# Batch 0's second token pair by seven products, one sink product for two heads, and a new order: windowed attention with sinks before a squared-ReLU layer pair

## The chip, the cores and the metric

The kernel runs on one core of a Trainium2 chip. The time is the device time in microseconds (us) of one execution; medians of runs are compared. The engines are called PE (TensorE: products; PEld: its weight loads), DVE (VectorE), ACT (ScalarE), POOL (GpSimd) and SP (SyncE, which here issues transfers).

## The reference

```python
batch, n_heads, seq, head_dim = (4, 8, 768, 64)
n_sink, window = (4, 128)

scores = scale * q @ k.T                       # per batch and head, scale = 1/sqrt(64)
keep = (column < n_sink) | (0 <= row - column < window)
a = softmax(where(keep, scores, -1e9))
x = (a @ v)                                    # -> [batch * seq, heads * 64] = [3072, 512]
h = x @ w_in                                   # [3072, 2048]
out = (relu(h) ** 2) @ w_out                   # [3072, 512], float32
```

(The lines are shortened from the reference; q, k and v are float32 of [4, 8, 768, 64].)

Attention is banded: a row sees 128 columns behind it and the first four columns of its batch, the sinks. Then come two dense layers with a squared ReLU between them.

## The kernel before

**Tiling.** A batch has 768 tokens, that is 6 tiles of 128 (t = 0 to 5), taken as 3 pairs (s or u = 0 to 2). Heads are taken in 4 pairs (m = 0 to 3), two of them at a time. Products are in bf16, sums in fp32 in the PSUM banks.

**Attention** (`attention`, from line 562). Queries and keys are turned, for batches 0 and 1 on PE (L642), for 2 and 3 by transposing transfers on SP (L596). Scores are products with 64 rows of contraction (L749), keys by queries, two heads in the two halves of the PE array. ACT takes the exponent into `expm` (L769); DVE or POOL masks the band's triangles (L778, L781, L360). The sinks' scores for all heads are one small group of products (`pk`, L708), and their exponents lie in `es`: heads in groups of four rows, so that one 128-row operand holds all heads. `vs` holds, for each head, the sinks' values (and a one for the row sum) in that head's rows and zero elsewhere. In `values` (L797 to L819) each head and token tile gets up to three products into 65 columns of a bank: previous tile, own tile, and, for t >= 2, the sinks (L815). Column 65 is the softmax's sum; DVE divides (L833, L834) into `xn_sb`. PE or a transfer turns that into `xT`, the input of the dense layers (L866 and its copies, L848).

**First layer** (`layer1`, L884). 16 blocks of 128 of the 2048 inner columns; products at L895 into `pm`, ReLU into `r` on ACT (L906) or DVE (L908), square into `gT` on DVE (L917) or ACT (L915).

**Second layer.** It exists in two forms, each for a pair of token tiles (256 tokens by 512 output columns, contraction 2048):
- `layer2` (L921): plain, 2 tiles by 16 blocks = 32 products of 512 columns (L936), then two copies of 128x512 to `osb`.
- `layer2_fast` (L981): one step of Winograd's form of Strassen's scheme. The pair is a 2 by 2 block matrix (tile by inner half), w_out another (inner half by column half). Seven block products of 8 products of 256 columns each (L1047) take the place of eight. Four sums of the left operand are made on DVE (L1005: s1 to s4; s3 in place in `gT`), four of w_out once for the kernel (`weight_sums`, L964, L977), and the results are combined by additions on DVE (L1072, L1088, L1095) and copies on ACT or DVE.

In the kernel before, pairs 0 and 1 of batch 0 go by `layer2` (in four parts by inner columns, `by_part=True`, L1193) and the other ten pairs by `layer2_fast`.

**The order of the work.** Nothing is ordered by the text of the program. Each step (a group of products, a copy, a load) is an `op` of a `Plan` (L152), with the engines that it may take, its planned cost on each, what it comes after and which buffers it takes and frees. `Plan.run` (L183) is a list scheduler: again and again it picks, of the ops that are ready, the one with the smallest planned start plus its own `lag`, and then the smallest `key`, gives it to the engine where it ends first, and emits it. A producer on another engine counts as ready LATENCY after its planned end (L222). `place` (L170) then moves the ops of a group, such as ('l2', b, u), by PLACES (shift of the key, scale of the key, lag), and single ops by NUDGES, which names them by their number in the list of ops (shift of the key, lag). So a changed number anywhere can change the order in all five queues. Loads keep their order within a queue (`follow`). Op 25 is the load of the third quarter of w_in, 24 and 26 those of the second and the fourth.

**Buffers.** The PSUM has two pools of two buffers each, `att` and `den` (L289); `sg` has four buffers for the sums of the fast form.

Of the kernel before, what the change touches and what calls it, by code (L numbers as in the profile page):

```python
# [16 lines left out]
LATENCY = 0.135  # L17
# [5 lines left out]
    ('att', 0, 0): (3.3, 1.08, 0.18), ('att', 0, 1): (3.285, 0.47, 0.38), ('att', 0, 2): (-0.2, 1.41, -0.24),  # L23
    ('att', 1, 0): (-1.415, 2.2, -0.42), ('att', 1, 1): (-0.385, 1.02, -0.22), ('att', 1, 2): (6.08, 1.06, 0.36),
    ('att', 2, 0): (-0.225, 0.25, -0.64), ('att', 2, 1): (-1.615, 1.17, -0.58), ('att', 2, 2): (0, 1.02, -0.06),
    ('att', 3, 0): (-0.075, 1.08, 0.1), ('att', 3, 1): (-0.04, 1.04, 0.04), ('att', 3, 2): (1.235, 0.72, 0.98),
    ('ev', 0, 2): (-0.16, 1.15, 0.78), ('ev', 1, 0): (0.585, 0.56, -0.48), ('ev', 1, 1): (0.47, 1.11, 0.24),
    ('ev', 1, 2): (-0.095, 1.18, 0.08), ('ev', 2, 0): (-0.22, 0.93, 0.28), ('ev', 2, 1): (0.015, 1.02, -0.46),
    ('ev', 2, 2): (1.345, 0.4, 1.32), ('ev', 3, 1): (-0.155, 1, 0.08), ('ev', 3, 2): (-0.055, 1.28, -0.44),
    ('l1', 0, 0): (-0.035, 1.27, 0), ('l1', 0, 1): (0.18, 0.85, 0.08), ('l1', 0, 2): (-0.6, 1.31, -0.4),  # L30
    ('l1', 1, 0): (4.96, 0.3, 0.74), ('l1', 1, 2): (0.265, 1.41, -0.28), ('l1', 2, 0): (-0, 0.59, 0.5),
    ('l1', 2, 2): (0.1, 1.22, -0.12), ('l1', 3, 0): (0.075, 0.91, 0.48), ('l2', 0, 0): (0.055, 0.81, 0.38),
    ('l2', 0, 1): (0.435, 1.16, 0), ('l2', 0, 2): (0.16, 1.12, -0.1), ('l2', 1, 0): (1.05, 0.56, -0.96),
    ('l2', 1, 1): (-0.425, 1.06, -0.1), ('l2', 1, 2): (-0.18, 1.03, 0.2), ('l2', 2, 0): (-0.115, 0.96, 0.58),
    ('l2', 2, 1): (2.185, 1.21, 1.32), ('l2', 2, 2): (2.75, 1, 0.74), ('l2', 3, 0): (-0.765, 0.25, 2.4),
    ('l2', 3, 1): (0.08, 0.81, 0.18), ('l2', 3, 2): (0.23, 1.94, 2.82), ('prep', 0, 0): (2.165, 1.2, -0.5),
    ('prep', 0, 1): (0.115, 1.01, -0.24), ('prep', 1, 0): (0.05, 0.87, 0.08), ('prep', 1, 1): (0.84, 1.23, 0.54),
    ('prep', 2, 0): (-0.005, 0.96, 0.24), ('prep', 3, 0): (-0.045, 1.08, 1.16),
    ('sink', 0, 0): (0.015, 1.11, -0.04), ('sink', 0, 1): (0, 1.12, -0.06), ('sink', 1, 0): (-0.225, 1.01, -0.06),
    ('sink', 3, 0): (-0.565, 0.62, 0.5), ('sum', 0, 2): (-0.14, 0.68, -0.34), ('sum', 1, 0): (-1.615, 0.44, -1.74),  # L40
    ('sum', 1, 1): (0.645, 0.91, -1.4), ('sum', 1, 2): (0.34, 1.45, 0.14), ('sum', 2, 0): (-0.655, 1.85, 0.06),
    ('sum', 2, 1): (-0.24, 1, 0.18), ('sum', 2, 2): (0.405, 1.27, 0.3), ('sum', 3, 0): (0.25, 2.36, 0.94),
    ('sum', 3, 2): (0.185, 1.17, 1.74), ('turn', 0, 0): (-0.56, 2.1, -0.62), ('turn', 0, 1): (0.11, 0.94, -0.14),
    ('turn', 0, 2): (-0.205, 1.01, 0.02), ('turn', 1, 0): (-0.2, 0.94, -0.02),
    ('turn', 1, 1): (-0.345, 1.33, -0.42), ('turn', 1, 2): (1.765, 2.5, -2.14), ('turn', 2, 0): (0, 1.05, 0),
    ('turn', 2, 1): (-0.26, 1.09, -0.3), ('turn', 3, 0): (-0.06, 1.05, -0.44), ('turn', 3, 1): (0.075, 0.56, 0.64),
    ('turn', 3, 2): (0, 1, 0.14), ('val', 0, 0): (0.345, 0.45, -0.28), ('val', 0, 1): (0.69, 0.58, -0.46),
    ('val', 0, 2): (-0.09, 0.78, -0.08), ('val', 1, 0): (-2.595, 0.7, 0.22), ('val', 1, 1): (0.035, 1.14, 0.06),
    ('val', 1, 2): (-0.65, 0.98, 0.64), ('val', 2, 0): (-1.11, 0.59, -1.94), ('val', 2, 1): (0.755, 0.42, -0.3),
    ('val', 2, 2): (-0.425, 1.6, -0.06), ('val', 3, 0): (0.1, 1.17, 0.6), ('val', 3, 1): (0.805, 0.25, 0.74),  # L50
    ('val', 3, 2): (0.105, 0.92, 2.28), ('wt', 0): (-0.205, 0.82, -0.32),
}
NUDGES = {
    4: (-0.022, 0.56), 16: (0, 0.14), 17: (-0.211, -0.38), 18: (0.48, -1.62), 19: (0, 0.4), 20: (0.364, -0.58),
    21: (0.004, 0.16), 22: (0.02, 0), 23: (0.016, 0.18), 24: (-0.06, -0.78), 25: (0.35, 1.84), 26: (-0.106, 0.66),
    27: (0.014, -0.64), 29: (-0.004, 0.86), 30: (0, 0.42), 31: (0.013, 0), 33: (-0.009, 0), 34: (-0.094, 0.5),
    36: (-0.027, 0.16), 37: (0.188, 0.08), 38: (-0.052, 0), 39: (-0.269, -0.82), 40: (-0.004, 0),
    41: (-0.419, 0.34), 42: (0.398, -2.86), 43: (0.134, -0.1), 44: (0.027, 0.14), 45: (0.009, 0), 46: (0.123, 0.66),
    47: (0.073, 0.9), 49: (0, 0.1), 51: (-0.102, -0), 52: (-0.278, -0.06), 53: (-0.001, 0.18), 56: (0.05, 0.1),
    57: (0.049, -0.16), 58: (0.016, -0.78), 60: (-0.008, -0.14), 61: (-0.013, 0), 62: (0, 0.22), 63: (-0.292, -0.2),  # L60
    64: (-0.079, 0.34), 65: (0.028, 0.64), 66: (-0.114, -0.38), 67: (0.099, -0.02), 68: (0.076, -0.28),
    69: (-0.851, 0.68), 71: (0.036, 0.22), 72: (-0.036, -0.24), 73: (0.024, 0.18), 74: (0.02, 0), 75: (-0.063, 0),
    76: (0, -0.04), 78: (0.042, 0.28), 80: (0.009, 0.26), 81: (0.023, 1.36), 82: (-0.02, 0.04), 83: (-0.008, -0.54),
    84: (-0.128, -0.42), 85: (-0.161, -0.36), 86: (0.003, 0), 87: (-0.004, 0.08), 88: (-0.069, 0),
    89: (-0.003, -0.16), 90: (-0.088, 0.02), 91: (0.016, -0.28), 92: (0.109, 0), 93: (0.015, 0.38),
    94: (0.043, -0.24), 95: (0.159, 0.04), 96: (-0.083, 0.04), 97: (-0.05, -0.3), 98: (-0.346, 0.8),
    99: (-0.435, 0.54), 100: (-0.21, -0.52), 101: (0.407, 1.44), 102: (0.013, 0.78), 103: (0.147, -0.08),
    104: (-0.112, -0.16), 105: (-0.121, -0.1), 107: (0.009, 0), 108: (0.214, 0.04), 109: (0.006, 0.08),
    111: (0.033, 0.86), 112: (0.046, 0.56), 113: (0.043, 0.6), 114: (-0.154, 0.42), 115: (-0.084, -0.16),
    116: (-0.145, -0.28), 117: (-0.026, -1.22), 118: (0.126, -0.62), 119: (-0.123, -0.24), 120: (0.115, 0.56),  # L70
    121: (0, -0.14), 122: (-0.121, 0.08), 123: (0, -0.2), 124: (0.034, -0.16), 125: (-0.168, 0.24),
    126: (0.017, -0.44), 127: (0.071, -0.82), 128: (-0.128, 0.1), 129: (-0.006, -0.08), 130: (0, -0.56),
    131: (0.402, 0.04), 132: (-0.056, 0), 133: (0.291, -0.28), 134: (-0.028, 0), 135: (0.064, -1.52),
    136: (-0.069, 0), 137: (-0.061, 0.54), 139: (-0.041, 0.32), 140: (-0.043, 0), 142: (-0.077, -0.12),
    143: (-0.069, 0.14), 144: (0.271, 0.26), 145: (0.008, 0.02), 146: (0.046, -0.52), 147: (0.008, -0.22),
    148: (0.006, 0.26), 149: (-0.028, 0.28), 150: (0.065, 0.06), 151: (0.051, 0.04), 152: (0.164, -0.12),
    153: (-0.401, 0.06), 154: (0.019, 0), 155: (-0.388, -0.64), 156: (-0.112, 1.16), 157: (0.287, 0.94),
    158: (-0.278, 1.3), 159: (-0.002, -0.18), 160: (0.118, 0.3), 162: (0.145, 0.5), 164: (0.158, 0.46),
    165: (0.095, 0), 166: (0.015, 0.02), 167: (0.055, 0), 168: (0.161, -0.48), 169: (-0.217, 0.24),
    171: (0.132, 0.52), 172: (0.011, -0.1), 173: (-0.036, 0.78), 174: (-0.047, -0.16), 175: (0.115, 0),  # L80
    176: (-0.342, 0.18), 177: (0, -0.02), 178: (-0.092, 0.58), 179: (0.041, 0.04), 180: (0.136, 0),
    186: (0.353, 0.28), 187: (-0.073, -0.02), 188: (-0.044, 0.48), 189: (-0.009, 0.06), 190: (0.057, -0.6),
    191: (-0.512, 1.18), 192: (0.405, 0.62), 193: (-0.012, -0.02), 194: (-0.003, 0.04), 195: (0.216, 0.94),
    196: (-0.08, -0.04), 197: (-0.038, 0.14), 198: (0.002, -0.54), 199: (0.12, 0.14), 200: (-0.304, 0),
    201: (-0.106, -0.12), 202: (0.038, 0.08), 203: (-0.001, -0.3), 205: (0.013, -0.44), 206: (-0.01, 0.46),
    207: (-0.003, 0.02), 208: (0.277, 0.98), 209: (0.006, -1.42), 210: (0.099, 0.36), 211: (0.041, 0),
    212: (0.006, 0), 214: (0.108, 0.54), 215: (0.057, 0.38), 216: (0.2, 0.22), 217: (-0.118, -0.12),
    218: (-0.002, 0.26), 219: (0.129, -0.22), 220: (0.008, -0.44), 221: (0.213, 1.02), 222: (0.464, -0.34),
    223: (-0.206, 0.1), 224: (0.064, 0), 225: (0.277, 0.32), 226: (-0.123, 0.62), 227: (0.015, 1.76),
# [170 lines left out]
def kernel(  # L260
# [301 lines left out]
    def attention(b, key):  # L562
# [16 lines left out]
        def stage(g, f0, f1, side):  # L579
# [9 lines left out]
            if b in NATURAL:  # L589
                for s in range(NS):  # L590
                    for ti in (1, 0):
                        for i in range(2):
                            t = 2 * s + i
# [641 lines left out]
```

The softmax here doesn't subtract the row's maximum and nothing guards it: scores larger than these inputs give would overflow.

## Time and profile before

Three runs: median 215.46 us, 214.94 to 216.12 us. The profiled execution spans 215.2 us from the first to the last instruction.

| engine | busy, us | share | instructions |
|---|---|---|---|
| PE | 208.1 | 97% | 2189 |
| PEld | 161.4 | 75% | 2189 |
| DVE | 147.0 | 68% | 282 |
| ACT | 118.9 | 55% | 149 |
| POOL | 78.7 | 37% | 112 |

By line of the chain that ended last: first layer (L895) 38% of the span, fast second layer (L1047) 28%, plain second layer (L936) 7%, values (L817) 6%, scores (L749) 5%, the load of w_in 5%.

| products | columns | number | mean latency, ns |
|---|---|---|---|
| first layer, L895 | 256 / 512 | 384 / 192 | 273 / 380 |
| plain second layer, L936 | 512 | 64 | 380 |
| fast second layer, L1047 | 256 | 544 | 273 |
| values, L817, from v | 65 | 352 | 193 |
| values, L817, sinks | 65 | 128 | 193 |

How to read it: the mean of a product in the profile is its latency from start to end; products overlap, so the pace is read from the starts in the timeline. "Busy" counts time with at least one such interval open. The chain of waits goes back from the last instruction to what released each step. All times in the timeline are counted from the first instruction.

### The profile page before, as it was taken

The numbers are of one execution on the slowest core, as the hardware profiler recorded it, in microseconds if no ns is written. First come the engines' busy times: TensorE is split into PE (matmuls) and PEld (weight loads), VectorE is DVE, ScalarE is ACT, GpSimd is POOL, SyncE is SP. The second block draws the span as 40 slices with busy tenths as digits, with TensorE's granted clock in tenths as the row PEclk, the third lists the DMA queues.
The fourth block names the chain that finished last, engine by engine and source line by source line (L and its number), as shares of the span: only waits on it lengthen the run. The fifth ranks groups of instructions, "written<-read, shape, count | busy, mean of one in ns | idle before, by whom it ended". The sixth has DMA issues, their size and how long they took to land.

```text
span 215.2 us, 5184 instructions
## 1 busy us (share of the span) xinstructions
PE 208.1 (97%) x2189; PEld 161.4 (75%) x2189; DVE 147.0 (68%) x282; ACT 118.9 (55%) x149; POOL 78.7 (37%) x112
## 2 busy tenths in 40 slices
PE   7997999999999999999999999999999999999993
PEld 7666997579587655679898965886997955798892
DVE  6586659568958875677778757648886654476853
ACT  3697356545764578977744369768306135671110
POOL 6989374399979840793900000000000100000000
PEclk9999999999999999999999999999999999999999
DMA  4999999999999999999999633000413260000222
GB/s 144 294 177 203 173 201 212 158 106 197 152 156 141 211 214 129 148 114 158 92 177 172 167 75 122 3 0 0 52 71 90 86 149 0 0 3 2 97 100 97
DMA packets 93351, 26.06 MB, mean 121 GB/s; under 512 B 86800, under 2 KB 91280, under 8 KB 93328
## 3 DMA queue, kind: packets, MB, share of 16 engines
q0 software_dynamic: 69248, 12.59, 81.3%
q1 hardware_dynamic: 23896, 13.07, 28.1%
q8 instruction: 17, 0.28, 0.6%
q10 hardware_dynamic: 184, 0.07, 0.1%
q14 instruction: 6, 0.05, 0.1%
HBM read 27.30 MB, written 6.29 MB: 156 GB/s over the span
## 4 chain that ended last, share of the span: by engine, by line
PE 90%; DMA 5%; ACT 2%; DVE 1%; POOL 1%; issue 0%; POOLq 0%
PE pm L895 38%; PE py L1047 28%; PE py L936 7%; PE po L817 6%; PE ps L749 5%; DMA w_in_sb<-in_moe_w_in_dram 5%; PE pt L642 3%; PE pt L327 2%; ACT expm L769 1%; PE ya L1047 1%; PE px L866 1%; DVE xT L336 1%; POOL expm L360 1%; PE pk L708 1%; ACT qs L334 0%
## 5 line engine op out<-in xcount | busy, mean ns | idle before, releaser
L895 PE MATMUL pm<-xT,w_in_sb 128*128 128x256 bf16 (+1 forms) x576 | 87.4, 309 | 0.7 <-DMA w_in_sb<-in_moe_w_in_dram 0.5
L895 PEld LDWEIGHTS <-w_in_sb 128*128 128x128 bf16 x576 | 62.4, 114 | 20.7 <-issue 1.3
L906 ACT ACTIVATE r<-pm 128x1024 bf16<-128x1024 f32 x42 | 43.0, 1024 | 33.8 <-PE pm L895 31.7
L769 ACT ACTIVATE expm<-ps 128x1024 bf16<-128x1024 f32 (+1 forms) x48 | 43.4, 953 | 15.5 <-PE ps L749 15.5
L917 DVE TENSOR_TENSOR gT<-r 128x1024 bf16<-128x1024 bf16 x35 | 24.2, 691 | 22.7 <-ACT r L906 22.6
L1047 PEld LDWEIGHTS <-gT 128*128 128x128 bf16 x336 | 31.1, 98 | 4.5 <-issue 1.2
L360 POOL TENSOR_SCALAR_AFFINE_SELECT expm<-expm 128x512 bf16<-128x512 bf16 x12 | 7.3, 632 | 73.6 <-ACT expm L769 68.6
L1047 PEld LDWEIGHTS <-sg 128*128 128x128 bf16 x240 | 22.9, 98 | 3.0 <-issue 0.5
L781 DVE TENSOR_TENSOR expm<-expm,tri 128x1024 bf16<-128x1024 bf16 x26 | 18.2, 705 | 7.7 <-ACT expm L769 7.5
L1047 PE MATMUL py<-wt,gT 128*128 128x256 bf16 x160 | 20.8, 273 | 0.0
L1047 PE MATMUL py<-wt,sg 128*128 128x256 bf16 x160 | 20.8, 273 | 0.0
L817 PE MATMUL po<-v,expm 128*128 128x65 bf16 x352 | 17.7, 193 | 1.1 <-DMA v<-in_v_dram 1.0
L1047 PE MATMUL py<-w_out_sb,gT 128*128 128x256 bf16 x144 | 18.7, 273 | 0.0
L817 PEld LDWEIGHTS <-expm 128*128 128x128 bf16 x352 | 16.5, 97 | 1.9 <-issue 0.4
L834 DVE TENSOR_TENSOR xn_sb<-po,rc 128x512 bf16<-128x512 f32 (+1 forms) x28 | 17.2, 615 | 1.0
L334 ACT ACTIVATE osb<-py 128x256 f32<-128x256 f32 (+1 forms) x15 | 6.6, 441 | 16.8 <-PE py L1047 11.7
L936 PE MATMUL py<-w_out_sb,gT 128*128 128x512 bf16 x64 | 15.6, 380 | 0.0
L749 PE MATMUL ps<-qkT 64*128 64x128 bf16 (+1 forms) x256 | 14.6, 238 | 0.0
L749 PEld LDWEIGHTS <-qkT 64*128 64x128 bf16 x256 | 8.0, 94 | 8.2 <-issue 7.6
L915 ACT ACTIVATE gT<-r 128x1024 bf16<-128x1024 bf16 x13 | 13.7, 1056 | 0.3
L817 PE MATMUL po<-vs,es 128*128 128x65 bf16 x128 | 13.0, 193 | 0.0
L817 PEld LDWEIGHTS <-es 128*128 128x128 bf16 x128 | 11.7, 97 | 1.1 <-issue 1.1
(78 smaller groups left out, 242.0 us busy)
## 6 DMA issues: line engine op xcount, KB each, us to landing
out_dram<-osb SPq DMA_DIRECT2D x11, 512.0 KB, 3.9
v<-in_v_dram POOLq DMA_DIRECT2D x24, 128.0 KB, 6.7
qn<-in_k_dram POOLq DMA_DIRECT2D x20, 128.0 KB, 7.6
qn<-in_q_dram POOLq DMA_DIRECT2D x20, 128.0 KB, 7.9
w_in_sb<-in_moe_w_in_dram POOLq DMA_DIRECT2D x4, 512.0 KB, 10.3
w_out_sb<-in_moe_w_out_dram POOLq DMA_DIRECT2D x4, 512.0 KB, 10.6
qr<-in_k_dram SPq DMA_DIRECT2D x4, 256.0 KB, 5.1
qr<-in_q_dram SPq DMA_DIRECT2D x4, 256.0 KB, 4.9
```

The costliest lines, as they stand in the source:

```text
L360: nc.gpsimd.affine_select(out=e_tile, in_=e_tile, compare_op=ALU.is_ge, fill=fill, base=i - 1, pattern=[[0, n], [1 if i else -1, 128]], ch ...
L749: nc.tensor.matmul(ps[:, h2, o:o + w], lhsT=qkT_sb[r, m, 1, c, :], rhs=qkT_sb[r, m, 0, qb:qb + w // 128, :], start=(i == 0 and not biased) ...
L769: nc.scalar.activation(out=x[:, :, o:512], in_=bank_t["s", b, s, m][:, :, o:512], func=AF.Exp, scale=scale)
L781: nc.vector.tensor_mul(y, y, tri.rearrange("p (o a) c -> p o (a c)", o=1).to_broadcast([128, 4, 256]))
L817: touch(("po", b, s, m0), e, nc.tensor.matmul(pv[:, i, h2, :], lhsT=lhsT, rhs=rhs, start=(n_ == 0), stop=(n_ == len(mms) - 1)), j)
L834: touch(("po", b, s, m0), e, nc.vector.tensor_tensor(out=xn_sb[:, 2 * s:2 * s + 2, 128 * (m0 + j0):128 * (m0 + j0 + nj)].rearrange("p i (j ...
L895: nc.tensor.matmul(pm[:, i, :], lhsT=w_in_sb[:, fb // 4, kb, fb % 4:512:4], rhs=xT[:, c0 // 256:(c0 + cw) // 256, kb, :], start=(kb == 0), ...
L906: nc.scalar.activation(out=o, in_=h, func=AF.Relu)
L915: nc.scalar.activation(out=g, in_=r, func=AF.Square)
L917: nc.vector.tensor_mul(g, r, r)
L936: touch((b, u), e, nc.tensor.matmul(pm[:, i, :], lhsT=gT_sb[t // 4][:, fb, 128 * (t % 4):128 * (t % 4) + 128], rhs=w_out_sb[:, fb, :], sta ...
L1047: ins = nc.tensor.matmul(y_, lhsT=x[:, i, :], rhs=r_, start=(first or tail and n == 2) and i == 0, stop=i == HB - 1, skip_group_check=not ...
```

## The change

There are three parts.

1. Pair 1 of batch 0 goes by `layer2_fast` instead of `layer2`. Pair 0 stays plain. The aim is fewer products on PE.
2. The sink products of the two heads of a pair become one: `es` is the same operand for both, so the two `vs` blocks of 65 columns are taken side by side, 130 columns, into the bank's two neighbouring regions. The aim is fewer PE instructions.
3. The order is new: LATENCY is 0.216 instead of 0.135, and all of PLACES and NUDGES are replaced by numbers that a search gave, one that was run with long lengths for PE's work. The planned costs in the program are as before.

```diff
-LATENCY = 0.135
+LATENCY = 0.216
 PE_SLACK = 0.0
...
 PLACES = {
-    ('att', 0, 0): (3.3, 1.08, 0.18), ('att', 0, 1): (3.285, 0.47, 0.38), ('att', 0, 2): (-0.2, 1.41, -0.24),
...
+    ('att', 0, 0): (1.285, 1.65, -0.18), ('att', 0, 1): (-0.055, 1.01, 0.04), ('att', 0, 2): (-0.37, 0.93, 0.26),
...
 NUDGES = {
...
-    21: (0.004, 0.16), 22: (0.02, 0), 23: (0.016, 0.18), 24: (-0.06, -0.78), 25: (0.35, 1.84), 26: (-0.106, 0.66),
...
+    24: (0.091, -0.2), 25: (0.016, -0.1), 26: (-0.055, -0.12), 27: (-0.054, 0.32), 30: (0.028, 0.5), 31: (0, 0.02),
...
@@ -811,8 +808,9 @@
                                         if t >= 1:
                                             mms.append((i, h2, x[:, h2, 256 * i:256 * i + 128], vb[:, t - 1, h, :]))
                                         mms.append((i, h2, x[:, h2, 256 * i + 128:256 * i + 256], vb[:, t, h, :]))
-                                        if t >= 2:
-                                            mms.append((i, h2, es[:, 128 * (t - 2):128 * (t - 2) + 128], vs[:, h, :]))
+                                        if t >= 2 and h2:
+                                            mms.append((i, slice(0, 2), es[:, 128 * (t - 2):128 * (t - 2) + 128],
+                                                        vs[:, 2 * m:2 * m + 2, :]))
...
@@ -1190,7 +1188,7 @@
         if b == 0:
             weight_sums(0.6, [w_out_op[i] for i in range(4)])
         for u in range(NS):
-            if b == 0 and u < 2:
+            if b == 0 and u < 1:
                 layer2(b, u, lambda i, part, u=u: 0.408 + 0.466 * (4 * part + 2 * u + i) / 24, by_part=True)
             else:
                 layer2_fast(b, u, lambda n, u=u, b=b: b + 0.5 + 0.5 * (8 * u + 8 * n / 7.0) / 24)
```

## The prediction

> **What bounds the kernel now.** I read the page first, parts 1, 2 and 4. They are these lines:
>
> ```profile
> span 215.2 us, 5184 instructions
> PE 208.1 (97%) x2189; PEld 161.4 (75%) x2189; DVE 147.0 (68%) x282; ACT 118.9 (55%) x149; POOL 78.7 (37%) x112
> ...
> PEclk9999999999999999999999999999999999999999
> DMA  4999999999999999999999633000413260000222
> ...
> PE 90%; DMA 5%; ACT 2%; DVE 1%; POOL 1%; issue 0%; POOLq 0%
> ```
>
> TensorE (PE) is on the chain for 90% of the span, at full clock. The single large other term is a transfer, 5%. Next I read the chain in order of time, to see where each of them stands:
>
> ```profile
> 13.83 9.99 DMA w_in_sb<-in_moe_w_in_dram
> 23.82 0.05 issue
> 23.87 7.18 PE pm L895 x64
> ...
> 54.91 1.73 PE py L936 x8
> ...
> 59.56 2.73 PE py L1047 x24
> ...
> 67.95 1.45 PE po L817 x48
> ...
> 74.54 0.77 DVE xT L336 x2
> 75.31 0.05 issue
> 75.36 1.92 PE pm L895 x8
> ```
>
> So there are three stretches. Until 23.87 us the loads rule. From 23.87 to 211.70 us the products follow one another almost without a break; the one visible gap is at 75 us, where batch 1's first layer waits for its transposed input xT. From 211.70 to 215.2 us the last copy and the last stores run. The waits of PE alone sum to 3.6 us, of which 1.5 us is the identity at the start and 0.2 us lies at 75 us.
>
> In the timeline I took the start-to-start distance of the products, since the durations in the groups are latencies that overlap: 8 products of 512 columns (L936) take 1.73 us, 216 ns each; 24 of 256 columns inside 6.11 us for 56 (L1047), 109.1 ns each; 24 of 65 columns (L817) take 0.725 us, 30.2 ns each; 16 transposes of 128 columns take 0.90 us, 56 ns each. Multiplying all products after 23.87 us by these gives about 184.4 us of the 187.8 us there. The slack of 3.4 us splits in about 0.8 us of gaps (75 us, 93 us) and 2.6 us of switches: each of the 24 visits to the 64-row score products costs its neighbours about 0.11 us (24 products at L1047 take 2.73 us beside a visit, 2.62 us otherwise).
>
> The groups by shape, duration after the comma, and busy time of the engines in two stretches (PE, PEld, DVE, ACT, POOL):
>
> ```profile
> L936 PE MATMUL py<-w_out_sb,gT 128*128 128x512 bf16 x64 | 15.6, 380 | 0.0
> L817 PE MATMUL po<-vs,es 128*128 128x65 bf16 x128 | 13.0, 193 | 0.0
> L1005 DVE TENSOR_TENSOR sg<-gT 128x1024 bf16<-128x1024 bf16 x10 | 6.9, 688 | 0.3 <-ACT gT L915 0.2
> ...
> 48.00:58.00 10.00, 10.00 (x98) 8.07 (x97) 8.68 (x14) 6.28 (x10) 9.70 (x12) 1.00 2.06 175
> 54.00:76.00 22.00, 21.81 (x268) 15.10 (x265) 17.42 (x38) 13.53 (x22) 19.22 (x24) 1.00 2.27 165
> ```
>
> The 64 products at L936 are the two plain second-layer pairs of batch 0; pair 1, the one changed, is the 32 that start at 54.74 us and end at 72.5 us. VectorE (DVE) is 79% busy between 54 and 76 us, 87% between 48 and 58 us with no gap on PE.
>
> **What the Trainium skill says.** "TensorE: Matmul & The Clock Gate", section "Back-to-back issue gap", gives N/2.4 + 2.5 ns for warm products of N columns: 29.6, 109.2 and 215.8 ns for 65, 256 and 512. The trace agrees (30.2, 109.1, 216). The same page, "Step-by-step: what each phase is for", says that weight loads are pulled ahead of running products. The trace agrees: 56 L1047 products, each with a load of 98 ns, keep 109.1 ns. And "Architectural detail: the array is 16× 32×32, not 1× 128×128" says that ScalarE and VectorE are strictly first in, first out; so an early-placed DVE instruction that waits holds all behind it. The trace shows such waits only as idle time (22.6 us of DVE at L917 on ScalarE), which costs nothing while PE runs on.
>
> **The change, part by part.**
>
> Pair 1 of batch 0. It removes 32 products of 512 columns: 32 × 216 ns = 6.91 us of PE. It adds 7 × 8 = 56 products of 256 columns: 56 × 109.1 ns = 6.11 us. PE saves 0.80 us, and both ends are measured, so this is sure as long as PE is the bound. Weight loads rise by 24 of 98 ns, hidden as above. On DVE it adds four sums of 8 × 128 elements at 0.69 us (2.76 us), three 256-column additions at 0.42 us (1.26 us) and the middle one at 0.69 us: 4.71 us. On ScalarE or DVE two copies of 0.60 us become three of 0.38 to 0.42 us: nothing. The store keeps its 512 KB.
>
> Its waits: the first product needs the first sum and the weight sums; those end at 51.6 us, before the pair began in the kernel before. The fourth product waits for the copy of the first (0.38 us, two products or 1.75 us in between), the sixth for an addition. Queued behind each on PE is whatever the order put next, and behind that attention of batch 1. Pair 2 already runs this way between 59.49 and 66.9 us without a gap, so I cost them at nothing, provided that DVE isn't late.
>
> Sinks. For token tiles 2 to 5, four head pairs and four batches, two products of 65 columns become one of 130: 64 times 2 × 30.2 = 60.4 ns against 130/2.4 + 2.5 = 56.7 ns by the section above (the nearest row, 128 columns, is 56 ns). That is 3.7 ns × 64 = 0.24 us. Bounds: 0 if the weight load sets the pace, 0.40 us if only the 54.2 ns of columns count. A product of 65 columns is already set by its columns, so halving the number of instructions brings little.
>
> The order. The planner's LATENCY goes from 0.135 to 0.216 us and all shifts are new; costs in the plan stay. The trace says the new figure fits products: the four transposes that start at 92.76 us are through by spacing at 92.98 us, and the copy they release starts at 93.19 us, 0.21 us later. (From DVE to PE it is 0.05 us.) A plan that knows the hop should leave fewer small gaps. What an order can win is bounded: 0.8 us of gaps and part of 2.6 us of switches after 23.87 us; before it, PE waits 1.4 us for v at 18.1 to 19.5 us, 0.3 us at 20.8 and 0.4 us at 23.0. I take a sixth of that 5.5 us, about 0.9 us, as won: an estimate, and the softest term. One readable shift is that of planned operation 25, the third quarter of w_in: its lag falls from 1.84 to −0.10, so GpSimd should issue it at about 11.5 us instead of 13.83 us, ahead of the triangle masks. I count nothing for it: the transfer is queued behind v and w_in's second quarter, which landed at 19.5 and 21.2 us.
>
> Sum: 215.46 − 0.80 − 0.24 − 0.9 = 213.5 us; rounded for what the gap at 75 us may take back (0.2 us), 213.7 us.
>
> **The rivals.**
>
> PE stays the bound and the order wins a part (my forecast): 213.7 us. For it: 90% of the chain on PE, DVE free enough elsewhere (72% from 75 to 126 us), and the sums need only the squares of tiles 2 and 3, so they can go before 54 us, or pair 2 can move behind 75 us.
>
> Given back: half of the added DVE work stays between 54 and 76 us. 17.42 + 2.36 = 19.8 us; at 90% that needs 22.0 us, as long as before. The shorter pair then only lengthens the wait at 75 us, and the sinks remain: 215.2 us. For it: the chain passes over DVE's copy to xT just there. Against: the order was made anew for it.
>
> DVE becomes the bound there: three quarters stay, 20.95 us at 90% is 23.3 us, 1.3 us more than before; 215.46 + 1.3 − 0.24 = 216.5 us; if all stays, 24.6 us and 217.8 us. For it: GpSimd, which could take masks, is 87% busy there with issuing loads. Against: ScalarE has 39% free and can take squares and copies.
>
> The start moves too: if w_in's third quarter really lands earlier, or v's wait is filled, up to 1.7 of the 2.1 us of waits before 23.87 us go: 213.7 − 1.7 = 212.0 us. For it: the DMA share in 16 to 22 us is only 62 to 69%. Against: the transfers run in queue order.
>
> **How the numbers follow.** Chances: forecast 0.46, start too 0.12, given back 0.18, DVE bound 0.24. The predicted time is the first, 213.7 us. The range reaches from the 212.0 us of the good start to 217.0 us, into the DVE case but not to its worst end. Faster by over 0.5% means below 214.4 us: nearly all of the first two cases, 0.57. Slower by over 0.5% means above 216.5 us: the DVE case as worked out begins there and goes to 217.8 us, so nearly all of it, 0.23. No change is the case of the gain given back and what is left of the others, 0.20.
>
> **What would show it.** Right: no L936 line for pair 1 (32 products left), L1047 up from 544 to 600 products of 256 columns, 64 sink products of 130 columns some 57 ns apart; L1005 up by four; the gap before batch 1's first layer no longer than 0.5 us; PE's end of work 1.0 to 2.0 us earlier than 211.7 us. Wrong: a longer chain piece over DVE (sums, masks, xT) between 50 and 80 us; a first unbroken stretch of layer 1 that begins well off 23.87 us, either way; or more visits to the score products than 24, at 0.11 us each. The forecast fails most likely in the order's term, which no view of the kernel before can size.

## The result, and the profile after

| | runs | median, us | lowest to highest, us |
|---|---|---|---|
| before | 4 | 215.28 | 214.94 to 216.12 |
| after | 4 | 218.15 | 217.78 to 218.36 |

The ratio of after to before is 1.0122, with a 95% interval of 1.0096 to 1.0148. A second comparison, on another chip, gave 217.36 us against 215.32 us, 1.0095 (1.0062 to 1.0127). So the change made the kernel slower by about 1%. The forecast was 213.7 us, with a range from 212.0 to 217.0 us.

The page of the kernel after, parts 1, 2 and 4 (busy time and share of each engine, the granted clock and the DMA share in 40 slices, the chain that ended last):

```profile
span 215.9 us, 5124 instructions
PE 206.1 (95%) x2149; PEld 162.6 (75%) x2151; DVE 146.6 (68%) x282; ACT 124.7 (58%) x154; POOL 83.2 (39%) x119
...
PEclk9999999999999999999999999999999999999997
DMA  5999999999999999999999671020118010000205
...
PE 73%; DMA 17%; POOL 6%; issue 1%; SPq 0%; DVE 0%; ACT 0%; POOLq 0%
```

PE is busy for 2.0 us less than on the page of before (206.1 against 208.1), and yet the span is no shorter. The granted clock is no cause: it is at 90% or more in every slice but the last, when PE is done, and its mean was 1.000 in the slowest of the four executions. On the chain PE has 73% where it had 90%; transfers have 17% where they had 5%. The chain in order of time shows which transfers (start, length, what):

```profile
27.46 12.82 DMA w_out_sb<-in_moe_w_out_dram
...
48.31 7.67 DMA qn<-in_q_dram
...
56.03 0.90 PE pt L639 x13
```

The chain no longer follows PE from 23 us on. Up to 56 us it follows GpSimd, which issues loads one by one, and two transfers: w_out, and the last load of batch 1's queries, which landed at 55.98 us. TensorE stood still for that load; this is the list of PE's waits (what waited, for what: us in total, times, longest):

```profile
PE pt L639 <- DMA qn<-in_q_dram: 1.1, 3, 0.7
```

The kernel before has no such line. The timeline of PE has the three gaps (start, us, operation, in brackets the idle time before it):

```profile
47.69 0.68 PE L639 MATMUL pt<-ident,qn 128*128 128x128 bf16 x9 [0.20 <-DMA qn<-in_q_dram]
...
55.09 0.23 PE L639 MATMUL pt<-ident,qn 128*128 128x128 bf16 x1 [0.17 <-DMA qn<-in_q_dram]
56.03 0.90 PE L639 MATMUL pt<-ident,qn 128*128 128x128 bf16 x13 [0.71 <-DMA qn<-in_q_dram]
```

A wait costs more than the idle time in brackets. The transpose at 55.09 us and the next one stand 0.94 us apart, where the pace is 0.056 us. So 0.88 us is lost, but only 0.71 us of it is idle, because the product before the wait is still shown as running for its latency of 0.23 us. Counted from start to start, the three waits cost 0.36, 0.33 and 0.88 us, together 1.57 us.

The two gaps of the kernel before, at 75 and at 93 us, are gone: the 512-column pieces of batch 1's first layer now begin only at 81.7 us, without a wait for xT.

At the other end, the timeline of SyncE, which issues the stores, of the kernel before (its first page) and of the kernel after:

```profile
200.49 6.45 SPq L1120 DMA_DIRECT2D out_dram<-osb  x2
```

```profile
199.74 0.33 SPq L1118 DMA_DIRECT2D out_dram<-osb  x1
...
211.37 0.42 SPq L1123 DMA_DIRECT2D out_dram<-osb  x1
211.88 0.38 SPq L1118 DMA_DIRECT2D out_dram<-osb  x1
```

The last instruction is a store at L1118, 512 KB: that of batch 3's pair 1. The kernel before issued both of its late 512 KB stores (L1120) before 207 us, and only smaller pieces after them. The new order puts the store of pair 1 behind the last pair's stores, although its data lay ready at about 208.6 us. From PE's end (210.94 us) to the end of the span it takes 4.96 us; in the kernel before, 3.5 us.

One of the groups by shape (count | busy us, mean ns of one | idle before) and two stretches by engine (PE, PEld, DVE, ACT, POOL, clock, DMA share, which passes 1 where packets overlap, GB/s):

```profile
L815 PE MATMUL po<-vs,es 128*128 128x130 bf16 x64 | 10.8, 220 | 0.0
...
48.00:58.00 10.00, 9.12 (x127) 7.08 (x126) 8.08 (x19) 6.34 (x10) 8.63 (x11) 1.00 2.44 181
54.00:76.00 22.00, 21.12 (x292) 18.61 (x289) 16.85 (x35) 17.17 (x23) 18.24 (x25) 1.00 2.12 157
```

The products are the ones that the change should give: 64 sink products of 130 columns, 600 products of 256 columns at L1045 (544 before), and at L934, the old L936, 32 weight loads left of 64. VectorE is busy for 16.85 us between 54 and 76 us, no more than before (17.42 us on the first page, 16.96 us in the later profile): it did not become the bound there. It is PE that is idle, 0.88 us in each of the two stretches, which share the gaps at 55 and 56 us.

### The profile page after: what moved, and what is told of

Read it like the earlier page. It is cut to its first block, busy times and chain, and to the rows that moved or that the text cites. A ratio compares the mean times of both kernels' runs of the same rounds, so it can differ in the third digit from the quotient of the medians.

```text
span 215.9 us, 5124 instructions
## 1 busy us (share of the span) xinstructions
PE 206.1 (95%) x2149; PEld 162.6 (75%) x2151; DVE 146.6 (68%) x282; ACT 124.7 (58%) x154; POOL 83.2 (39%) x119
## 4 chain that ended last, share of the span: by engine, by line
PE 73%; DMA 17%; POOL 6%; issue 1%; SPq 0%; DVE 0%; ACT 0%; POOLq 0%
PE pm L893 33%; PE py L1045 28%; DMA w_out_sb<-in_moe_w_out_dram 6%; PE po L815 5%; DMA w_in_sb<-in_moe_w_in_dram 5%; PE ps L746 4%; DMA qn<-in_q_dram 4%; POOL v L518 2%; DMA qr<-in_k_dram 2%; POOL qn L509 2%; POOL vs L687 1%; PE pt L639 1%; PE ya L1045 1%; POOL w_out_sb L453 1%; PE px L864 1%
## 5 line engine op out<-in xcount | busy, mean ns | idle before, releaser
L904 ACT ACTIVATE r<-pm 128x1024 bf16<-128x1024 f32 x45 | 46.1, 1024 | 31.6 <-PE pm L893 30.8
L1045 PEld LDWEIGHTS <-gT 128*128 128x128 bf16 x368 | 34.2, 98 | 4.7 <-issue 0.6
L915 DVE TENSOR_TENSOR gT<-r 128x1024 bf16<-128x1024 bf16 x31 | 21.4, 691 | 23.5 <-ACT r L904 23.5
L1045 PEld LDWEIGHTS <-sg 128*128 128x128 bf16 x264 | 25.4, 98 | 3.1 <-issue 0.2
L357 POOL TENSOR_SCALAR_AFFINE_SELECT expm<-expm 128x512 bf16<-128x512 bf16 x18 | 11.7, 687 | 29.3 <-ACT expm L766 20.0
L1045 PE MATMUL py<-wt,gT 128*128 128x256 bf16 x176 | 22.9, 273 | 0.0
L1045 PE MATMUL py<-wt,sg 128*128 128x256 bf16 x176 | 22.7, 273 | 0.0
L1045 PE MATMUL py<-w_out_sb,gT 128*128 128x256 bf16 x160 | 20.7, 273 | 0.0
L913 ACT ACTIVATE gT<-r 128x1024 bf16<-128x1024 bf16 x17 | 17.8, 1055 | 2.9 <-DVE xT L333 2.6
L547 POOL DMA_DIRECT2D v<-in_v_dram x12 | 10.7, 899 | 5.4 <-PE py L1045 2.5
L1045 PE MATMUL py<-w_out_sb,sg 128*128 128x256 bf16 x88 | 11.4, 273 | 0.0
L537 POOL DMA_DIRECT2D qn<-in_q_dram x12 | 10.7, 903 | 1.6 <-DMA qn<-in_k_dram 1.3
```

The source lines that it names most:

```text
L357: nc.gpsimd.affine_select(out=e_tile, in_=e_tile, compare_op=ALU.is_ge, fill=fill, base=i - 1, pattern=[[0, n], [1 if i else -1, 128]], ch ...
L537: return [nc.gpsimd.dma_start(out=qn_t[b, ti][:, t, :].rearrange("p (h d) -> p h d", d=D), in_=(q, k)[ti][b, :, 128 * t:128 * t + 128, :]. ...
L904: nc.scalar.activation(out=o, in_=h, func=AF.Relu)
L913: nc.scalar.activation(out=g, in_=r, func=AF.Square)
L915: nc.vector.tensor_mul(g, r, r)
L1045: ins = nc.tensor.matmul(y_, lhsT=x[:, i, :], rhs=r_, start=(first or tail and n == 2) and i == 0, stop=i == HB - 1, skip_group_check=not ...
```

## The experiments

All times are compared with the kernel before on the same chip. In several of them the planner's search is replaced by a written list of its operations with their engines (`ORDER`, taken from the plan of one of the two kernels, then edited), so that only what is named differs.

### The kernel before once more

No edit. The page of before, on which the prediction rests, is of an execution of 217.03 us, 1.6 us over the median, so another profile was wanted.

> The kernel before, unchanged, for a profile of a usual execution: the first profile of it has a span of 215.2 us in an execution of 217.03 us, while its median is 215.28 us, so a usual span should be about 1.8 us shorter. If the first profile was late at the start (loads), the long unbroken stretch of products begins nearer 22 us than 23.87 us and ends near 210 us. If it was late elsewhere, the stretch begins at 23.8 us and a gap behind it is missing. Either way the tail behind the last product stays 3.5 us.

Measured: 215.55 us, span 213.8 us. The unbroken stretch of layer 1 begins at 22.43 us (23.87 us on the first page), PE ends at 210.25 us, and the rest is as on the first page, shifted by 1.44 us. From here on "before" means this profile. Three terms make up its span: 22.43 us to the stretch, 187.82 us from there to PE's end, 3.55 us to the end of the last store. In after they are 22.91, 188.03 and 4.96 us: +0.48, +0.21 and +1.41, together the 2.1 us of the two spans. The medians are 2.87 us apart in the first comparison and 2.04 us in the second, so up to 0.8 us of the first is not accounted for by these two executions.

### The late store alone

```diff
-            op(key(6), {"sp": 0.1}, store, after=[em, e1, e4], reads=[os_], dma=2.0)
+            ops["store", b, u] = op(key(6), {"sp": 0.1}, store, after=[em, e1, e4], reads=[os_], dma=2.0)
...
+    ops["store", 3, 1].lag = 0.0
```

> The changed kernel with one edit: the 512 KB store of batch 3's pair 1 is placed ahead of the last pair's small stores on SyncE instead of behind them; all other queues are as in the changed kernel. Theory A (the new order put a large store at the very end): the tail behind the last product shrinks from 5.0 to about 3.5 us, so 218.15 - 1.4 = 216.7 us, ratio to before about 1.007. Theory B (the time is lost in the middle, by the seven-product pair's VectorE work or by waits): at most 0.2 us, ratio 1.012.

Measured: 216.92 us, ratio 1.0046 (1.0025 to 1.0067), and when it was run again as a partner (below) 216.27 us, 1.0035 (1.0014 to 1.0056). Of 1.0095 to 1.0122 between 0.5 and 0.9% is gone, 1.1 to 1.9 us, depending on which runs are paired. The profile of the second run shows it more sharply: PE ends at 210.22 us, the span at 213.8 us, 3.6 us instead of 4.96, and it is 3.6 us in the first run's profile too. The queues of the other four engines are the same. So the late store costs the 1.4 us, as the profile of after said.

### The two parts alone

Merged sinks in the kernel before, all queues in the order of before:

```diff
-                                        if t >= 2:
-                                            mms.append((i, h2, es[:, 128 * (t - 2):128 * (t - 2) + 128], vs[:, h, :]))
+                                        if t >= 2 and h2:
+                                            mms.append((i, slice(0, 2), es[:, 128 * (t - 2):128 * (t - 2) + 128],
+                                                        vs[:, 2 * m:2 * m + 2, :]))
```

> The kernel before with only the sink products of two heads joined; the order in all queues is that of before, 64 products fewer. By columns: 64 times 3.7 ns = 0.24 us less, 215.0 us, ratio 0.999. If the weight load set the pace of these products, nothing or up to 64 times 30 ns = 1.9 us less (ratio 0.991) since half of the sinks' loads go. If joining costs anything, above 1.000.

Measured: 215.30 us, 0.9993 (0.9972 to 1.0014), which alone would settle nothing. The chain in order of time does (first this kernel, then before: a values piece, and the step behind the last product):

```profile
38.97 1.42 PE po L818 x40
...
209.73 0.02 issue
```

```profile
39.32 1.45 PE po L817 x48
...
210.25 0.02 issue
```

Eight merged products save 0.03 us, about 4 ns each, where 3.7 ns was forecast. From the stretch of layer 1 (22.09 us here) to PE's end it is 187.64 us, 0.18 us less than before; 56 of the 64 merged pairs lie behind the stretch's start, and 56 times 3.7 ns is 0.21 us.

The new order without either part: the order of after as a list, with pair 1 plain in the places that the fast form has there, and the sinks apart. No sums and combining additions for pair 1.

```diff
-            if b == 0 and u < 1:
+            if b == 0 and u < 2:
...
-    P.place(PLACES)
-    P.run()
+    P.replay()
```

> The changed kernel's order with both other parts undone: pair 1 of batch 0 plain in the places of the seven products, and sink products apart; the order is replayed, so all else stands where it stands in the changed kernel. If the parts save what was reckoned and PE is the bound everywhere: 218.15 + 0.80 + 0.24 = 219.2 us, ratio 1.018. If the pair's saving ends in the wait for batch 1's last loads at 55 us (1.1 us in the changed kernel's profile), the longer pair only shortens that wait: 218.15 + 0.2 = 218.4 us, ratio 1.014. If the parts are what costs, below 217 us.

Measured: 217.47 us, 1.0088 (1.0057 to 1.0120). This is after's result without the parts of the change that save products. The stretch of layer 1 starts at 22.38 us, PE ends at 210.84 us: 188.46 us, 0.64 us more than before; PE waits 0.78 us for the same loads. The list of its waits:

```profile
PE pt L893 <- DMA qn<-in_q_dram: 0.8, 2, 0.6
```

Both kernels have to be counted alike, with every wait taken out from start to start. Before has two, those for xT at 73.9 and 92.2 us in this profile, which cost 0.37 and 0.31 us: 187.82 less 0.68 leaves 187.14 us. The new order has neither of them. It has 1.11 us of waits for batch 1's loads and 0.30 us of two others: 188.46 less 1.40 leaves 187.06 us. So the order closed the two old gaps, 0.7 us, and won less than 0.1 us on switches, and it opened 1.4 us of new waits.

### The wait for batch 1's loads: is it there again, and can PE do something else?

After once more, beside the next two:

> The changed kernel once more, on the same chip as the two below: 218.1 us, ratio 1.012. If its first measurement was unlucky in its loads, nearer 217 us.

Measured: 217.36 us, 1.0095 (1.0062 to 1.0127). PE is idle for 0.57 us at 47.3, 0.20 us at 54.7 and 0.65 us at 55.6 us, 1.42 us in sum; from layer 1 to PE's end it takes 188.36 us. The waits are not an accident of one execution.

The transposes that wait moved behind the values and one piece of batch 0's layer 1, on top of the early store:

```diff
 ORDER
-    (248, 'pe'), (249, 'act'), (251, 'pe'), (252, 'act'), (253, 'dve'), ... (180, 'pe'), (181, 'act'),
+    ... (180, 'pe'), (181, 'act'), (248, 'pe'), (249, 'act'), (251, 'pe'), (252, 'act'), (253, 'dve'),
```

> The changed kernel with the early store and a second edit: on PE (and on ACT and DVE behind it) the turning of batch 1's last queries and keys, which waits for their loads at 55 to 57 us, stands behind three products (values, layer 1) that are ready by then. Theory A (the order believes the loads earlier than they are, and PE waits): the wait of 1.1 to 1.8 us goes, so about 1.1 us less than with the early store alone, near 215.7 us, ratio 1.002. Theory B (PE has nothing else to do there, and the wait only moves to the next product): no change, ratio 1.005.

Measured: 219.23 us, 1.0183 (1.0145 to 1.0221), slower than after, though the wait for the loads at 55 us is gone. The timeline of PE in this kernel:

```profile
48.34 0.68 PE L900 MATMUL pt<-ident,qn 128*128 128x128 bf16 x9 [1.63 <-DMA qn<-in_q_dram]
...
62.27 0.40 PE L1007 MATMUL ps<-qkT 64*128 64x128 bf16 x6 [0.90 <-ACT expm L1027]
```

PE now waits for ScalarE (0.90 us at 62.3 and 0.52 us more at 63.2 us), and the first gap is 1.63 us in this execution. The edit put layer 1's ReLU ahead of the copies of the transposes in ScalarE's queue, and PE then waited for exponents. It shows that work for PE was there, and that moving one step by hand opens the next wait; it doesn't size the wait of the loads.

### Why the loads are late

Batch 1's q and k loads and its v loads are issued by GpSimd, each 128 KB, one in 0.88 us. Ahead of the last two q loads, at 46.66 us in after, SyncE issues the store of pair 0, 512 KB. In this experiment the store moves behind that of pair 1 in SyncE's queue; the early store of batch 3 is in both.

```diff
 ORDER
-    (288, 'sp'), ... (307, 'sp'), (381, 'sp'),
+    ... (307, 'sp'), (288, 'sp'), (381, 'sp'),
```

> The changed kernel with the 512 KB store of batch 3's pair 1 issued when its data is ready, as in the earlier run of the same edit, here as the partner of the next kernel on the same chip. Both theories: about 216.4 us, 1.0046 of the kernel before, with 1.1 to 1.8 us of PE waiting for batch 1's q load near 47 and 55 us.

> As store_early_again, and the 512 KB store of batch 0's pair 0, issued near 47 us ahead of the q and k loads of batch 1, goes behind the store of pair 1 near 56 us; nothing but the order of SyncE's queue differs. Theory A, the loads are late because they share the transfers' throughput with that store (512 KB at 175 GB/s by the share between 48 and 58 us are 3.0 us[...]): the last q load lands 1 to 1.5 us earlier, the waits of PE near 55 us fall from 0.85 to at most 0.3 us, and the time by 0.5 to 1.0 us against its partner: ratio 1.000 to 1.002. Theory B, the loads are late because of when and how they are issued (GpSimd's and SyncE's queue, latency): the landing and the waits stay, ratio 1.0046 as its partner.

Measured: the partner 216.27 us, 1.0035 (1.0014 to 1.0056); with the store moved 215.66 us, 0.9997 (0.9975 to 1.0019). That is 0.6 us, though the two intervals overlap a little; the traces say more. From the stretch to PE's end: 188.20 us in the partner, 187.26 us here. The load's piece in the chain, partner first:

```profile
47.71 7.64 DMA qn<-in_q_dram
```

```profile
48.37 6.78 DMA qn<-in_q_dram
```

It takes 0.86 us less, but it is issued 0.66 us later in this execution, so it lands only 0.2 us earlier; layer 1 began 0.93 us later too. After itself is the better partner here: the last two k and two q loads of batch 1 are issued there within 0.06 us of the same times, and land 0.68 to 0.83 us later than with the store moved. That is less than the 1 to 1.5 us expected. The idle time of PE at the loads falls from 1.37 us in the partner to 0.40 us. The transfers between 49 and 53 us, by queue (packets, MB, share), in after:

```profile
q0 software_dynamic: 3009, 0.38, 165.5%
q1 hardware_dynamic: 142, 0.52, 38.0%
```

and with the store moved:

```profile
q0 software_dynamic: 4600, 0.58, 309.1%
```

GpSimd's loads (q0) move 0.58 MB in these 4 us when they are alone, and 0.38 MB beside the store (q1). Two other kernels with the store moved (below) have 0.58 MB as well, and the kernel before, which also stores 512 KB at that time, has 0.37 MB. The Trainium skill says it in "DMA: Bandwidth & Descriptors", section "Issuing engines are not separate DMA queues": transfers that different engines issue run on the same 16 DMA engines and interleave. The trace agrees. Theory A holds in kind, with a smaller size; theory B falls.

The loads could also be helped from GpSimd's side. In the new order batch 1's first v tile is needed only at 74 us, so its load can go behind the last q load:

```diff
 ORDER
-    (45, 'pool'), (46, 'pool'), ... (52, 'pool'), (53, 'pool'),
+    (46, 'pool'), ... (52, 'pool'), (45, 'pool'), (53, 'pool'),
```

> store_moved, and the load of batch 1's first v tile, which the new order needs only at 74 us, goes behind batch 1's last q load on GpSimd; nothing else differs. Each load takes GpSimd 0.88 us to issue. Theory A, loads land in the order and at the pace of their issue: the last q load lands 0.7 to 0.9 us earlier than in store_moved (issue at about 47.3 us against 48.4), the wait of PE at 55 us goes (0.16 us there), the one near 47.5 us stays (its load is issued ahead of the moved one): 0.1 to 0.3 us less than store_moved, ratio 0.998 to 1.000. From the first unbroken stretch of layer 1 to PE's end 187.0 us (before 187.80, less 0.98 of the two parts, plus what is left of the waits). Rival: the landing is set by the bytes in the queues, no change against store_moved.

Measured: 216.12 us, 1.0017 (0.9997 to 1.0036). The wait at 55 us is gone, as expected; nothing is won by it in the median. PE's waits in this execution:

```profile
PE po L1076 <- POOL expm L618: 0.7, 1, 0.7
PE pt L900 <- DMA qn<-in_q_dram: 0.7, 1, 0.7
```

The load that PE needs at 48 us is 0.70 us late here (0.24 us with the store moved alone), and at 62 us there is a new wait of 0.71 us for a mask on GpSimd, which stands in GpSimd's queue behind the loads. The last q load was issued at 47.91 us instead of 48.37, but it landed at 54.89 us instead of 55.15, 0.26 us sooner where 0.7 to 0.9 us was expected, and counted from the start of layer 1 no sooner (0.03 us). PE came to it later, having lost more at 48 us. So the theory of the landing is not borne out, and the rival, that the bytes in the queues set it, is not refuted.

### Does the new order lose at the start?

v_late, with everything planned before 24 us in the order of the kernel before:

> v_late, and everything planned before 24 us in the order of the kernel before, on all engines: the same set of TensorE steps, in the old sequence. Theory A, the new order also lost at the start (its stretches of layer 1 began at 22.0 to 22.95 us against 22.1 to 22.4): 0.3 to 0.5 us less than v_late, ratio 0.996 to 0.998, stretch from 22.1 to 22.5 us. Theory B, the start differs only from execution to execution with the landing of the first loads: the same as v_late within 0.2 us.

Measured: 216.05 us, 1.0023 (1.0004 to 1.0042), the same as v_late within the noise; with intervals of 0.4 us to either side a gain of 0.3 us is not excluded. The stretch began at 22.51 us, against 22.72 us. That is nearer to theory B: the 0.48 us of the start in the two profiles is not shown to be the order's. The stretch began anywhere from 22.02 to 22.95 us in the executions of the new order, from 22.09 to 23.12 us in those with the old one, and at 23.87 us on before's first page.

### The fast pair in the old order

The rival in which VectorE becomes the bound was tried in the order of before: pair 0 plain in pair 1's early places, pair 1 fast in pair 0's late places, its four sums right behind the weight sums, the sinks apart.

```diff
-            if b == 0 and u < 2:
+            if b == 0 and u < 1:
...
 ORDER
-    (276, 'dve'), (277, 'dve'), (190, 'dve'),
+    (276, 'dve'), (277, 'dve'), (289, 'dve'), (291, 'dve'), (292, 'dve'), (290, 'dve'), (190, 'dve'),
```

> The kernel before's order, replayed, with one part of the change: pair 1 of batch 0 by seven products in the late places of the plain pair 0 (53 to 71 us), and plain pair 0 in the early places of plain pair 1 (36 to 47 us). Sinks apart, as before. If PE stays the bound, 0.80 us less: 214.6 us, ratio 0.996. If the 4.7 us of added VectorE work between 49 and 75 us hold PE up, the saving is given back: ratio 1.000 up to 1.006 (1.3 us).

Measured: 217.97 us, 1.0112 (1.0091 to 1.0133). From the stretch to PE's end it takes 190.07 us, 2.25 us more than before, where the spacing of the products says 0.80 us less. The chain passes over VectorE:

```profile
51.86 0.69 DVE sg L1266
52.55 0.60 DVE gT L1266
53.15 1.14 DVE r L1169
54.29 0.34 DVE qkT L597
...
54.67 0.61 PE pt L903 x8
```

Four sums, from 50.4 us on, stand ahead of a ReLU and a copy that PE waits for. Between 48 and 58 us VectorE is busy 9.75 us of 10, and PE 8.88:

```profile
48.00:58.00 10.00, 8.88 (x98) 7.93 (x96) 9.75 (x17) 5.77 (x8) 9.10 (x11) 1.00 2.11 178
```

From start to start PE loses 1.4 us at 53 to 55 us, and 1.9 us more at 72 to 77 us, behind VectorE's divisions and copies and ScalarE's copies.

The same with the sums spread over spots where VectorE idled, that ReLU and one copy on ScalarE, and the combining additions later:

```diff
 ORDER
-    (198, 'dve'), (185, 'dve'), (202, 'dve'), (276, 'dve'), (277, 'dve'), (289, 'dve'), (291, 'dve'), (292, 'dve'), (290, 'dve'), (190, 'dve'),
+    (289, 'dve'), ... (291, 'dve'), ... (198, 'dve'), (185, 'dve'), (202, 'dve'), (292, 'dve'), (276, 'dve'), (277, 'dve'), (290, 'dve'), ... (190, 'act'),
```

> The order of the kernel before with pair 1 in the fast form late and pair 0 plain early, as in pair_in_old, but with the four sums spread over spots where VectorE idled instead of all behind the weight sums, one ReLU and one copy moved to ScalarE, and the combining additions later; order on PE, GpSimd and SyncE as in pair_in_old. Theory A, the loss of pair_in_old (1.0112) is VectorE's load between 48 and 58 us: the 0.9 us wait near 53.6 us goes, and at least half of the 2.4 us loss, ratio at most 1.006; below 1.000 only if the pair's 0.8 us also survives the wait for xT near 74 us. Theory B, the fast form itself costs PE more than the spacing says (visits, weight loads, waits inside it): ratio stays at 1.009 to 1.012.

Measured: 217.11 us, 1.0083 (1.0062 to 1.0103): between the two theories, and by its time nearer to B's 1.009 than to A's 1.006. The stretches (columns as above) say where:

```profile
48.00:58.00 10.00, 10.00 (x111) 9.18 (x109) 8.09 (x15) 7.78 (x13) 10.00 (x12) 1.00 2.15 182
54.00:76.00 22.00, 20.85 (x278) 16.75 (x276) 16.79 (x38) 12.93 (x23) 18.92 (x23) 1.00 2.45 160
```

The first place is healed: PE has no gap from 48 to 58 us, with the fast form running there. From the stretch to PE's end it takes 188.70 us, 1.37 us less than with the sums in a row. The second place remains: PE is idle for 1.15 us between 54 and 76 us, 0.41 us at 73.3 and 0.59 us at 74.8 us behind ScalarE's copies, and the chain from 67.4 to 75.3 us runs over VectorE's divisions and combining additions and ScalarE's copies. Theory B falls: with the waits taken out from start to start, 2.24 us, the stretch takes 186.46 us, and 187.14 us less the pair's 0.80 us is 186.34 us, so PE pays for the fast form what the spacing says. In these two placings in the old order the pair's gain is lost to the queues of VectorE and ScalarE, first at 54 and then at 74 us.

## Why the prediction was wrong

**The accounting.** From the start of the layer-1 stretch to PE's end, with the waits of PE of over 0.12 us, each counted from start to start (spots where the profile lacks the record of a product are left out). The last column is before's 187.14 us less what the spacing gives for the parts in that kernel: 0.80 us for the pair, 0.21 us for the sinks.

| kernel | measured, us | all waits | of these for batch 1's loads | without waits | by spacing |
|---|---|---|---|---|---|
| before | 187.82 | 0.68 | 0 | 187.14 | |
| merged sinks alone | 187.64 | 0.83 | 0 | 186.81 | 186.93 |
| order without the parts | 188.46 | 1.40 | 1.11 | 187.06 | 187.14 |
| after | 188.03 | 2.01 | 1.57 | 186.02 | 186.13 |
| after again | 188.36 | 2.22 | 1.93 | 186.14 | 186.13 |
| early store, first run | 189.23 | 3.09 | 2.80 | 186.14 | 186.13 |
| early store, second run | 188.20 | 2.16 | 1.87 | 186.04 | 186.13 |
| the same, transposes moved | 190.87 | 5.06 | 1.79 | 185.81 | 186.13 |
| early store, pair 0's store moved | 187.26 | 1.23 | 0.73 | 186.03 | 186.13 |
| the same, v late | 188.64 | 2.63 | 1.45 | 186.01 | 186.13 |
| the same, old start | 187.61 | 1.70 | 0.43 | 185.91 | 186.13 |
| fast pair in the old order | 190.07 | 3.80 | 0 | 186.27 | 186.34 |
| the same, sums spread | 188.70 | 2.24 | 0 | 186.46 | 186.34 |

The last two columns agree within 0.12 us, but for 0.22 us with the old start and 0.32 us with the transposes moved. So the pair's 0.80 us and the sinks' 0.21 us are in the changed kernel: without its waits it takes 1.0 us less than the order without the parts. They are swallowed by waits that the new order brought.

**Step by step.**

- *Pair 1: 0.80 us saved, sums and additions at nothing.* Right in size and right that VectorE isn't the bound, for another reason than the one given. The step took the 32 products from 54.74 us on for pair 1. They were pair 0's: in the plan of the kernel before, pair 1 stands from 35.2 to 46.1 us and pair 0 from 53.6 to 71.1 us, and the runs in the old order were built on that. So the sentence that the weight sums end before the pair began was false for the kernel before: pair 1 there began at 36.26 us. The new order puts plain pair 0 early and the fast pair at 43.4 us. Its sums stand from 34.6 to 39.4 us, in time that VectorE had free.
- *Sinks: 0.24 us.* Right. Most of after's sink products, 130 columns, stand 56 to 62 ns before the next product; the forecast had estimated 56.7 ns by the formula of the Trainium skill, "TensorE: Matmul & The Clock Gate", section "Back-to-back issue gap". Alone they brought 0.18 us where 0.21 us was to be had.
- *The order: about 0.9 us won, a sixth of 5.5 us.* This is the step that failed, and it failed by what it left out. What it put in came about: behind the start of layer 1 the new order closed the two gaps and won a little on switches, nearly 0.8 us. (That a sixth of all the slack came so near is luck: what was won is nearly all of the gaps and next to nothing of the rest.) But the forecast called the term soft and gave it a range on the winning side only; it put what a new order can lose at nothing, without a reason. The order lost 1.1 us (without the parts) to 1.6 or 1.9 us (after, twice) at the loads of batch 1, 0.3 to 0.4 us at other waits, and 1.4 us at the last store. The transposes of tiles 4 and 5 of batch 1 moved ahead, before first:

```profile
71.57 1.06 PE L642 MATMUL pt<-ident,qn 128*128 128x128 bf16 x16
```

```profile
54.64 0.28 PE L639 MATMUL pt<-ident,qn 128*128 128x128 bf16 x2
```

  The last load for them landed at 55.98 us. In the kernel before it landed even later, at 56.60 us, beside a store of the same size, and cost nothing, since it was not needed for another 15 us. The plan of the new order has that landing about 2 us too early (54.7 us on its clock, 54.0 on the page's), so the order that looks seamless to the planner is not on the chip.
- *Op 25, nothing.* Right: w_in's third quarter moved up, and layer 1 did not start earlier.
- *0.2 us back at 75 us.* That wait is gone; those at 47 to 56 us are the larger ones in its place.
- *Switches.* The score products are visited 24 times behind the start of layer 1 in both kernels, so the sign of more visits did not come.
- *Slack before 23.87 us.* That part of the 5.5 us was overstated: the page was of an execution that began its stretch 1.44 us later than the next one. And the DMA share of 62 to 69% in 16 to 22 us, the argument that the start could move too, was misread: the views of that profile give 1.24 to 1.37 for the three stretches of 2 us, and those are shares, not us. The DMA line of its page, too, has 90% or more there.

**The rivals.** None was right. "Given back" came nearest in kind: a wait takes the parts' gain away, but at the loads, not at xT. "VectorE becomes bound" has the nearest time, 216.5 to 217.8 us, and fails in after by its own measure (16.85 us of VectorE between 54 and 76 us, not 20 to 22). It is what happens to the pair in the old order in the two placings tried; that no placing there would do is not shown.

**What stays open.** The early store with pair 0's store moved ends PE 0.56 us sooner, from the stretch on, than before, and yet the two kernels' times are the same (0.9997, 0.9975 to 1.0019). The stretch began 0.52 us later in that execution; whether the new order delays it on the mean isn't shown; the run with the old start gives no sign of it, within its noise. How much of the waits a landing time of the right size in the plan would have avoided was not tried. No version was found that beats both kernels.

## What to carry to other kernels

A change that comes with a new order has two prices: its parts can be costed by spacing, but the order must be costed by asking which operation moved ahead of which load, and what the slack of that load was. Here the plan's own landing time was 2 us off for the load that mattered; where a new order uses a load 17 us sooner, look at what else moves bytes at that time, stores of a few hundred KB above all. And look at what stands last in the queue that ends the kernel: one large store there cost 1.4 us, more than both parts of the change could win. Last, count a wait on PE from start to start, in both kernels: by the idle times alone, and in the new order only, it seems as if the order had won 0.1 us, where it had won nearly 0.8 us and lost more.

## What was not expected of the hardware

- The same kernel before ranged from 214.54 to 216.89 us over 40 runs on one chip. Two profiles of it differ almost only at the start: the layer-1 stretch began at 22.43 us in one and at 23.87 us in the other, each time at the landing of w_in's third quarter, and everything behind it was alike. That the whole range comes from there is not shown.
- The four sums of pair 1 took 0.69, 1.00, 1.00 and 2.17 us in after, where the same shapes take 0.69 us elsewhere (medians over eleven). GpSimd ran masks and issued loads beside them. The Trainium skill, "SBUF — State Buffer", section "SBUF: two separate sides", says that VectorE and GpSimd share a pair of ports as an exclusive lock; the trace is consistent with it, but no run here tests it.
